# A block-sparse attention and expert-layer kernel on one core: mask step, a split cast and a new instruction order

## The chip, the cores and the metric

The kernel runs on one core of a Trainium2 chip. The metric is the device time of one execution in microseconds. The engines are TensorE (PE in the profile; PEld is its weight load), VectorE (DVE), ScalarE (ACT), GpSimd (POOL) and SyncE (SP), which only issues transfers here. Each engine works through its own instructions in the order of the program; they meet through semaphores.

## The reference, cut to what matters

```python
# 4 batches, 8 heads, 768 positions, head dimension 64; blocks of 32, so 24 blocks
scores = scale * q @ k.transpose(0, 1, 3, 2)
mask = abs(blk_i - blk_j) <= 1                       # the block's neighbours
mask |= (blk_i == 0) | (blk_j == 0) | (blk_i == 23) | (blk_j == 23)
for qb in range(24):                                 # three sampled blocks per query block
    for kb in sampled_blocks[qb]:
        mask[rows of qb, columns of kb] = True
attn = softmax(where(mask, scores, -1e9))
x = (attn @ v) as 3072 tokens x 512
h = x @ w_in                                         # 512 -> 1024
solu = h * softmax(h)
ln = (solu - mean) / sqrt(var + 1e-6) * g_ln
out = ln @ w_out                                     # 1024 -> 512
```

## The kernel before, in words

**Tiling.** Attention runs over 4 batches, 3 query tiles of 256 positions and 4 pairs of heads: 48 steps (`attend`). Each has three score groups (`score/b.t.pair.n`, L523: four matmuls of 256 columns into one of two `s` buffers of two banks each), three exps on ScalarE (`exp/...`, L528, 128 x 1024 each, into eight `ex` buffers) and one `pv` of 24 matmuls (L542). VectorE divides (`recip` L551, `norm` L554). A score group needs the transposed K and Q (`kT`, `qT`). The mask is added inside the score matmul: K and Q carry 24 extra rows, a selector of the key's block and -30000 where the query's block may not see that block.

**Opening and crossing.** For batch 0 (`opening`), SyncE loads K, Q and V of each pair (`load2` are 2 of the 6 chunks, `load4` the other 4, `load6` all), GpSimd or ScalarE casts them to bf16 next to the extra rows (`cast2`, `cast4`, `cast6`, L426), TensorE transposes them (`turn4`, `turn8`, L439) and VectorE copies the result out of PSUM (`evac4`, `evac8`, L426). `opening_rest` does the same for the other four chunks of Q (L484). Later batches (`crossed`) are cast by GpSimd (L495), transposed by a DMA that SyncE issues (`cross_kq`, L497) and split into `kT` and `qT` by VectorE (L501). GpSimd also casts V (L418).

**Expert layer.** Each of 24 feeds of 128 tokens (`feed`) does: two halves of `feed4` (L602, 512 columns), exp with its sum on ScalarE (`silu_e`, L624), the product on VectorE (`mult`, L627), statistics (`stats`, `aggr`), a small chain on GpSimd (`z2`, `vr`, `rs`: L640, L643, L676), a transposition of `u` by DMA (`cross_u`, L707) or on TensorE (first and last two), two halves of `out4` (L717), a scale by `rs` on VectorE (L723) and the store. Attention's result `x` is transposed by DMA (`cross_x`) or TensorE. The last two feeds are cut finer (`half_e`, `half_m`, `half_s`, `outh`), with a longer chain on GpSimd before `rs`.

**The mask step.** VectorE builds a 24 x 24 table of allowed block pairs: the fixed part (`allow0`, L280 and L282), then for each of the three samples one instruction that compares the block index with the sample and takes the maximum with the table so far (L287), the last of them writing `allow_b` in bf16. `maskmm2` and `maskmm4` (L305) spread it over positions, and L309 turns it into the extra rows of `qc` and `qr`.

**Order.** Nothing is scheduled automatically. Every operation is recorded in `Plan` in program order and numbered; `ORDER` lists the numbers in the order in which they are emitted, for all engines together, so it fixes each engine's queue. It also fixes which buffer of a pool an operation gets: the one that came free first. `SPARES` are matmuls of constants (L774) of the given column counts that compute nothing that is used; `ORDER` places them too.

Of the kernel before, what the change touches and what calls it, by code (L numbers as in the profile page):

```python
# [7 lines left out]
FP32 = mybir.dt.float32  # L8
# [6 lines left out]
SPARES = (512, 512, 512, 256, 256, 256, 256, 128, 128, 128, 128, 128, 128, 128, 128, 128, 128, 128, 128)  # L15
ORDER = [
# [107 lines left out]
def kernel(  # L124
# [11 lines left out]
    nc = tc.nc  # L136
# [678 lines left out]
```

## Time and profile before

| | |
|---|---|
| median of three runs | 207.87 us (207.56 to 208.7) |
| the profiled execution | 207.91 us |
| its span, first to last instruction | 206.2 us |
| TensorE busy | 198.3 us |
| ScalarE busy | 170.5 us |
| VectorE busy | 146.8 us |
| GpSimd busy | 73.0 us |
| moved by DMA | 41.29 MB |

The page gives an engine's busy time over the whole span; windows give it by stage. A timeline line has start, length, engine, line of the kernel, operation, output<-inputs, shapes and count; the bracket is the idle time of the engine ahead of it and what ended it. SPq is an issue on SyncE's queue, whose length is that of the issue alone. In a list of the chain of waits each line has start, length and what the chain ran through. A matmul's length holds its latency, so successive matmuls overlap: four score matmuls of 0.60 us follow each other every 0.44 us.

### The profile page before, as it was taken

The numbers are of one execution on the slowest core, as the hardware profiler recorded it, in microseconds if no ns is written. First come the engines' busy times: TensorE is split into PE (matmuls) and PEld (weight loads), VectorE is DVE, ScalarE is ACT, GpSimd is POOL, SyncE is SP. The second block draws the span as 40 slices with busy tenths as digits, with TensorE's granted clock in tenths as the row PEclk, the third lists the DMA queues.
The fourth block names the chain that finished last, engine by engine and source line by source line (L and its number), as shares of the span: only waits on it lengthen the run. The fifth ranks groups of instructions, "written<-read, shape, count | busy, mean of one in ns | idle before, by whom it ended". The sixth has DMA issues, their size and how long they took to land.

```text
span 206.2 us, 5792 instructions
## 1 busy us (share of the span) xinstructions
PE 198.3 (96%) x2292; PEld 141.3 (69%) x2292; DVE 146.8 (71%) x327; ACT 170.5 (83%) x210; POOL 73.0 (35%) x153
## 2 busy tenths in 40 slices
PE   3999999999999999999999999999999999999993
PEld 1888887677667667667666766666767676676452
DVE  6367489999897776877859374689586556459853
ACT  4298999999879898998888979998988999997570
POOL 6865423334516366311430415424120301200281
PEclk9999999999999999999999999999999999999999
DMA  4999999999999999999999969957972444342333
GB/s 134 294 333 373 283 285 253 257 216 223 162 315 305 280 198 278 197 328 207 281 294 184 227 181 279 177 130 80 209 163 51 103 104 80 79 105 51 74 118 120
DMA packets 71088, 41.29 MB, mean 200 GB/s; under 512 B 52236, under 2 KB 67092, under 8 KB 71060
## 3 DMA queue, kind: packets, MB, share of 16 engines
q1 hardware_dynamic: 69968, 39.86, 82.1%
q0 software_dynamic: 1056, 1.05, 3.0%
q8 instruction: 18, 0.29, 0.6%
q14 instruction: 10, 0.08, 0.2%
q10 hardware_dynamic: 36, 0.00, 0.0%
HBM read 23.07 MB, written 6.29 MB: 142 GB/s over the span
## 4 chain that ended last, share of the span: by engine, by line
PE 67%; DMA 15%; POOL 7%; issue 4%; DVE 4%; SPq 1%; ACT 0%; POOLq 0%; DVEq 0%; ACTq 0%
PE spairs L523 22%; PE mbank L717 16%; PE hpair L602 15%; PE mbank L542 12%; DMA qst<-in_q_dram 5%; DMA kst<-in_k_dram 4%; DMA vst<-in_v_dram 3%; DMA kx<-kb 3%; POOL kb L495 1%; PE sones L602 1%; SPq L497 1%; POOL va L418 1%; DVE u L654 1%; POOL rs L676 1%; DVE ot L723 1%
## 5 line engine op out<-in xcount | busy, mean ns | idle before, releaser
L528 ACT ACTIVATE ex<-spairs 128x1024 bf16<-128x1024 f32 x144 | 141.3, 1023 | 21.8 <-PE spairs L523 19.0
L523 PE MATMUL spairs<-qT,kT 88*128 88x256 bf16 x576 | 84.4, 274 | 0.9 <-ACT ex L528 0.6
L523 PEld LDWEIGHTS <-kT 88*128 88x128 bf16 x576 | 53.2, 98 | 21.6 <-issue 1.8
L717 PE MATMUL mbank<-w_out_sb,uT 128*128 128x512 bf16 x184 | 47.1, 379 | 0.0
L602 PE MATMUL hpair<-w_in_sb,xT 128*128 128x512 bf16 x176 | 45.0, 379 | 0.0
L542 PEld LDWEIGHTS <-ex 128*128 128x128 bf16 x1152 | 41.4, 97 | 4.7 <-DVE x L554 0.4
L542 PE MATMUL mbank<-va,ex 128*128 128x65 bf16 x1152 | 43.0, 193 | 0.0
L627 DVE TENSOR_TENSOR u<-hpair,e 128x1024 bf16<-128x1024 f32 x22 | 26.8, 1219 | 13.1 <-ACT e L624 12.9
L634 DVE BATCH_NORM_STATS2 bs<-u 128x6 f32<-128x512 bf16 x44 | 29.0, 678 | 0.2
L602 PEld LDWEIGHTS <-xT 128*128 128x128 bf16 x192 | 18.4, 97 | 13.7
L717 PEld LDWEIGHTS <-uT 128*128 128x128 bf16 x184 | 17.4, 97 | 13.5 <-DMA uT<-u 0.3
L723 DVE TENSOR_SCALAR ot<-mbank,rs 128x512 f32<-128x512 f32 x23 | 17.2, 747 | 11.2 <-POOL rs L676 6.9
L624 ACT ACTIVATE e<-hpair 128x1024 bf16<-128x1024 f32 x22 | 22.5, 1022 | 1.3 <-PE hpair L602 0.7
L643 POOL TENSOR_SCALAR vr<-z,mv 128x1 f32<-128x1 f32 x22 | 6.1, 280 | 44.9 <-DVE mv L637 35.2
L554 DVE TENSOR_TENSOR x<-mbank,r 128x256 bf16<-128x256 f32 x48 | 19.9, 414 | 0.8
L640 POOL TENSOR_TENSOR z<-z 128x1 f32<-128x1 f32 x22 | 4.2, 194 | 45.7 <-ACT e L624 41.3
L418 POOL CAST va<-vst 128x768 bf16<-128x768 f32 x16 | 14.6, 910 | 14.1 <-DMA vst<-in_v_dram 13.9
L551 DVE RECIPROCAL r<-mbank 128x4 f32<-128x4 f32 x48 | 8.4, 175 | 14.6 <-PE mbank L542 14.4
L676 POOL TENSOR_TENSOR rs<-vr,neg_half 128x1 f32<-128x1 f32 x24 | 13.5, 563 | 1.0
L495 POOL CAST qb<-qst 128x768 bf16<-128x768 f32 x12 | 10.2, 856 | 7.5 <-DMA qst<-in_q_dram 6.0
L495 POOL CAST kb<-kst 128x768 bf16<-128x768 f32 x12 | 10.4, 871 | 3.2 <-DMA kst<-in_k_dram 3.0
L501 DVE COPY kT<-kx 64x768 bf16<-64x768 bf16 x24 | 9.2, 383 | 2.2 <-DMA kx<-kb 1.8
(90 smaller groups left out, 122.6 us busy)
## 6 DMA issues: line engine op xcount, KB each, us to landing
vst<-in_v_dram SPq DMA_DIRECT2D x16, 384.0 KB, 5.2
out_dram<-ot SPq DMA_DIRECT2D x23, 256.0 KB, 3.0
kst<-in_k_dram SPq DMA_DIRECT2D x15, 384.0 KB, 4.7
qst<-in_q_dram SPq DMA_DIRECT2D x12, 384.0 KB, 4.8
w_out_f<-in_moe_w_out_dram SPq DMA_DIRECT2D x2, 1024.0 KB, 11.4
qst<-in_q_dram SPq DMA_DIRECT2D x4, 256.0 KB, 7.5
w_in_sb<-in_moe_w_in_dram POOLq DMA_DIRECT2D x2, 512.0 KB, 11.4
q0st<-in_q_dram SPq DMA_DIRECT2D x4, 128.0 KB, 3.9
```

What stands on the lines that cost most here:

```text
L418: ready_v[(b, pr)] = op(f"cast6/v{b}.{pr}", "POOL", lambda o: nc.gpsimd.tensor_copy(out=va[i][:, 2 * pr : 2 * pr + 2, :, 0:D], in_=vst[ld. ...
L495: ca = op(f"cast6/{nm}{b}.{pr}", "POOL", lambda o: nc.gpsimd.tensor_copy(out=cb[o.slot], in_=st[ld.slot].rearrange("p h c d -> p c h d")), ...
L523: nc.tensor.matmul(s[:, m, :], kT[0:KR, sl, jc, hh, :], qT[0:KR, sl, 2 * t : 2 * t + 2, hh, :], start=(m % 2 == 0), stop=(m % 2 == 1))
L528: exs.append(op(f"exp/{b}.{t}.{pr}.{n}", "ACT", lambda o, so=so: nc.scalar.activation(out=exb[o.slot], in_=banks("s", "pairs")[so.slot], f ...
L542: nc.tensor.matmul(acc(o)[:, qt, hh, :], exb[exs[n].slot][:, m, qt * P : (qt + 1) * P], va[i][:, 2 * pr + hh, jc, :], start=first, stop=(n ...
L554: nrm = op(f"norm/{b}.{t}.{pr}", "DVE", lambda o: nc.vector.tensor_tensor(out=xb[x_of[b, t].slot][:, :, 2 * pr * D : (2 * pr + 2) * D].rea ...
L602: nc.tensor.matmul(hb(n) if last else hb()[:, n, :], xTb[xt[0].slot][:, qt, c, :], w_in_sb[n][:, c, :], start=(c == 0), stop=(c == KD - 1))
L624: zs = op(f"silu_e/{j}", "ACT", lambda o: nc.scalar.activation(out=eb[o.slots["e"]], in_=hb().rearrange("p a f -> p (a f)"), func=ACT.Exp, ...
L627: us = op(f"mult/{j}", "DVE", lambda o: nc.vector.tensor_mul(out=ub[o.slot], in0=hb().rearrange("p a f -> p (a f)"), in1=eb[zs.slots["e"]] ...
L634: bs.append(op(f"stats/{j}.{n}", "DVE", lambda o, n=n: nc.vector.bn_stats(out=bsb[(bs[0] if bs else o).slot][:, n, :], in_=ub[us.slot][:, ...
L717: nc.tensor.matmul(mbank[m0.slot], uTb[ut[0].slot][:, KF // 2 * n + f, :], w_out_sb[n][:, f, :], start=(n == 0 and f == 0), stop=(n == 1 a ...
L723: fo = op(f"scale/{j}", "DVE", lambda o: nc.vector.tensor_scalar(out=otb[o.slot], in0=mbank[os_[0].slot], scalar1=rsb[rs.slot], scalar2=No ...
```

## The change

Three things change at once.

1. The mask table is built by two instructions instead of three: one comparison of the block index with all three samples (24 x 72 elements), written beside the fixed part into one bf16 tile, and one maximum over those four.
2. The second pair's K (batch 0, pair 1) is cast in two pieces on GpSimd, chunks 0 and 1 and then chunks 2 to 5, each with its own readers, where it was one cast of six chunks. For the pairs cast in one piece `ready_k` no longer names the first transposition for the second score group.
3. `ORDER` and `SPARES` are replaced: 14 spares of 4,352 columns instead of 19 of 4,096. Every operation keeps its engine.

```diff
-SPARES = (512, 512, 512, 256, 256, 256, 256, 128, 128, 128, 128, 128, 128, 128, 128, 128, 128, 128, 128)
+SPARES = (512, 512, 512, 512, 512, 256, 256, 256, 256, 256, 128, 128, 128, 128)
 ORDER = [
-    1124, 0, 21, 31, 1115, 2, 115, 11, 32, 1114, 3, 4, 5, 13, 33, 12, 14, 22, 15, 86, 9, 6, 16, 35, 23, 17, 18,
...
+    1120, 0, 5, 31, 2, 3, 30, 20, 21, 34, 23, 32, 4, 6, 13, 11, 9, 113, 17, 117, 10, 14, 22, 37, 12, 15, 115, 18,
...
 ]
...
-    allow = [const.tile([NB, NB], FP32, name=f"allow{i}") for i in range(3)]
+    allow = const.tile([NB, NR + 1, NB], BF16, name="allow")
...
-        out=allow[0], in0=dist, scalar1=1.0, scalar2=edge[1], op0=ALU.subtract, op1=ALU.is_le), [d2, e1])
-    static = op("small", "DVE", lambda o: nc.vector.memset(allow[0][:, 0 : NB : NB - 1], 1.0), [al0])
+        out=allow[:, NR, :], in0=dist, scalar1=1.0, scalar2=edge[1], op0=ALU.subtract, op1=ALU.is_le), [d2, e1])
+    static = op("small", "DVE", lambda o: nc.vector.memset(allow[:, NR, 0 : NB : NB - 1], 1.0), [al0])
...
-    prev, dep = allow[0], [static, iof, slo]
-    for r in range(NR):
-        nxt = allow_b if r == NR - 1 else allow[1 + r]
-        al = op("allow", "DVE", lambda o, r=r, prev=prev, nxt=nxt: nc.vector.scalar_tensor_tensor(
-            out=nxt, in0=iota_f, scalar=samp_f[:, r : r + 1], in1=prev, op0=ALU.is_equal, op1=ALU.max), dep)
-        prev, dep = nxt, [al]
+    eq = op("allow", "DVE", lambda o: nc.vector.tensor_tensor(
+        out=allow[:, 0:NR, :], in0=iota_f.rearrange("p (o b) -> p o b", o=1).broadcast_to([NB, NR, NB]),
+        in1=samp_f.rearrange("p (r o) -> p r o", o=1).broadcast_to([NB, NR, NB]), op=ALU.is_equal), [iof, slo])
+    al = op("allow", "DVE", lambda o: nc.vector.tensor_reduce(
+        out=allow_b, in_=allow.rearrange("p r b -> p b r"), op=ALU.max, axis=mybir.AxisListType.X), [eq, static])
...
+        elif (b, pr) == (0, 1):
+            ck = cast("POOL", kc, kst, 0, 2, lk, None, "kc", [lk], [lk])
+            cr = cast("POOL", kc, kst, 2, NCH, lk, ck, None, [lk], [lk])
...
-        ready_k[b, pr] = [[ga], [gr], [gr]] if first else [[ga], [ga, gr], [gr]]
+        ready_k[b, pr] = [[ga], [gr], [gr]]
```

By names, the start of three queues in the old and the new order:

```
TensorE before: spare128 spare512 spare512 maskmm2 turn4/k0.0 spare256 spare128 spare512 spare128 turn4/q0.0
                turn8/k0.2 spare128 turn4/q1.0 score/0.0.0.0 score/0.0.0.1 spare128 turn8/k1.2 turn4/k1.0
                score/0.0.0.2 turn8/k2.2 score/0.0.1.0
TensorE after:  spare256 turn4/k0.0 spare512 spare512 spare256 maskmm2 spare256 maskmm4 turn4/q0.0 turn8/k0.2
                score/0.0.0.0 turn4/q1.0 score/0.0.0.1 spare512 score/0.0.0.2 turn4/k1.0 turn8/k1.2 score/0.0.1.0
SyncE before:   k0(2) q0(2) k0(4) g q1(2) k1 k2 k3 v0 q2(2) q3(2) v1 q0(4) w_out q1(4) q2(4) v2 v3 k1.0 q3(4)
SyncE after:    q0(2) k0(2) q1(2) k0(4) q2(2) g q3(2) q0(4) k1 k2 v0 k3 v1 v2 w_out q1(4) v3 q2(4) q3(4) w_out k1.0
GpSimd after, from its first cast: q1(2) sel4 sel4 k0(4) maskc2 q2(2) q0(4) half maskc4 k1(2) k1(4) k2 v0 ... k3
```

In these lists `k1(4)` is the load or cast of four chunks of pair 1's K in batch 0, `k1` of all six, and `k1.0` the K of pair 0 in batch 1. Further on, the scores, exps and matmuls of the expert layer stand in nearly the same sequence; `out4/12` comes 732 ns of matmuls nearer to `feed4/12.1` (about 7.5 instead of 8.3 us of matmuls between them), and at the end `half_s/22.1` stands one place earlier on ScalarE and `rs/22` directly before `rs/23` on GpSimd, after `vr/23`.

102 rows, old and new, of the table ORDER are left out of this document.

## The prediction

> **What bounds the kernel now.** I read the page's busy shares and slices first, then the windows by stage, then the timeline of the first 26 us, the chain that ended last, and the timeline of the end.
>
> ```profile
> span 206.2 us, 5792 instructions
> PE 198.3 (96%) x2292; PEld 141.3 (69%) x2292; DVE 146.8 (71%) x327; ACT 170.5 (83%) x210; POOL 73.0 (35%) x153
> ...
> DMA  4999999999999999999999969957972444342333
> ```
>
> ```profile
> 9.40:33.70 24.30, 23.73 (x366) 20.77 (x364) 16.31 (x39) 22.55 (x26) 11.59 (x18) 1.00 1.10 302
> 33.70:57.00 23.30, 22.82 (x281) 16.40 (x280) 22.26 (x47) 21.62 (x27) 9.42 (x13) 1.00 1.13 227
> 57.00:190.00 133.00, 133.00 (x1539) 92.88 (x1536) 93.21 (x205) 117.43 (x138) 38.99 (x79) 1.00 0.85 189
> ```
>
> From 57 to 190 us TensorE is busy all 133 us: there the end moves only with TensorE's work, and the reordering changes none of it. Time can be won or lost in three places: before 57 us, where ScalarE (22.55 of 24.30 us) and the DMA engines (share 1.10) are nearly full too; at new holes between 57 and 190; and in the last 15 us.
>
> ```profile
> 1.30 0.45 SPq L332 DMA_DIRECT2D q0st<-in_q_dram  x1
> 3.65 0.50 DVE L287 SCALAR_TENSOR_TENSOR allow<-iota_f,samp_f,allow 24x24 f32<-24x24 f32 x2
> 4.18 0.23 DVE L287 SCALAR_TENSOR_TENSOR allow_b<-iota_f,samp_f,allow 24x24 bf16<-24x24 f32 x1
> 4.47 0.20 PE L305 MATMUL mbank<-allow_b,selp 24*128 24x24 bf16 x2 [2.52 <-DVE allow_b L287]
> ...
> 7.72 1.88 PE L523 MATMUL spairs<-qT,kT 88*128 88x256 bf16 x8
> ...
> 8.09 0.83 POOL L426 CAST kc<-kst 128x768 bf16<-128x768 f32 x1 [0.59 <-DMA kst<-in_k_dram]
> ...
> 8.81 4.17 ACT L528 ACTIVATE ex<-spairs 128x1024 bf16<-128x1024 f32 x4 [4.22 <-PE spairs L523]
> ```
>
> ```profile
> 11.96 2.85 ACT L528 ACTIVATE ex<-spairs 128x1024 bf16<-128x1024 f32 x3
> ...
> 17.82 1.04 PE L523 MATMUL spairs<-qT,kT 88*128 88x256 bf16 x8
> ```
>
> TensorE has nothing but spares until 4.47 us, then runs without a gap, but slowly: eight score matmuls take 1.88 us at 7.72 and 1.04 us at 17.82. The matmul records double their rate at 9.42. Exps follow each other every 0.915 us ((2.85 - 1.02) / 2). The 25th exp (third query tile, first pair) starts at 33.65, 24.84 us after the first; 24 x 0.915 = 21.96, so ScalarE waited 2.9 us in all. The second pair's K was issued at 3.19 and landed at 8.04.
>
> ```profile
> 15.60 9.73 DMA qst<-in_q_dram
> ...
> 29.40 8.46 DMA kst<-in_k_dram
> ...
> 48.09 6.09 DMA kx<-kb
> ```
>
> ```profile
> 200.61 0.56 POOL L676 TENSOR_TENSOR rs<-vr,neg_half 128x1 f32<-128x1 f32 x1
> 201.21 0.75 DVE L723 TENSOR_SCALAR ot<-mbank,rs 128x512 f32<-128x512 f32 x1 [1.51 <-POOL rs L676]
> ```
>
> The chain is transfers until 54 us, and TensorE's matmuls stand still for 0.11 us at 54.6 and 0.28 at 55.7 at its end. At the very end VectorE waits 1.51 us for `rs` of tile 22, and the last half product (`outh/1`) starts 0.5 us after `outh/0`'s last matmul for that.
>
> **The change part by part, against the profiled execution's 207.91 us (206.2 of span and 1.7 around it; the median of the three runs is 0.04 lower).**
>
> *Mask step: 0.* Three instructions of 0.23 us go. The new comparison has 72 elements a partition, between the 24x24 product at L274 (0.16) and twice L309's 96 elements (0.52); the maximum reads 96, likewise. Nearest is L309: 0.26 each. Together 0.3 to 1.0 us against 0.8, so `allow_b` comes between 0.5 us earlier and 0.3 later than 4.42. In the new order its first reader stands behind the first K transposition and three spares, 1,280 columns at the slow rate (0.107 us per 128): 1.07 us after about 5.05, so at 6.1. These hide either bound; without them the step would be worth its 0.5 or -0.3.
>
> *Order, first 12 us: +0.05 at the fourth exp.* SyncE now sends Q0 first, K0 second (issue 1.30; the second load landed at 4.17). K0's cast ends near 4.6 and TensorE starts at 4.65 with K0's transposition instead of the mask. Then 0.43 (four transpositions) + 1.07 (spares) + mask; `maskq` is 0.26 plus about 0.25 of latency, so Q0's transposition runs at 6.65 to 7.08, K0's other eight to 7.93 (0.85), first score at 7.93 against 7.72, first exp at 9.02 against 8.81 (1.09 after its score, as before). More hangs on the second K. `q0st` has two buffers, so Q2's load waits for Q0's cast (3.6) and Q3's for Q1's cast on GpSimd (about 5.0); Q3, the rest of Q0, K1 follow: K1 is issued at 5.95 instead of 3.19, and behind it in SyncE's queue K2, V0, K3, V1 all slide. Landing: small loads took 2.3 to 3.2 us, K1 4.85 and K2 5.32 in a full queue. With only 384 KB ahead I take 3.9: 9.85. GpSimd's two casts, 0.4 and 0.6 (L426 rows of 256 and 512 elements), end at 10.25 and 10.85; two transpositions, score, latency: 10.85 + 0.05 + 0.45 + 0.45 + 0.17 = 12.0 for the fourth exp, against 11.96. Cast in one piece (0.83) K1 would be done at 10.7, so the split itself is worth 0.1 either way.
>
> A page of the Trainium skill bears on that landing. "DMA: Bandwidth & Descriptors" (section "Anatomy of one DMA") gives about 2.0 us fixed plus bytes over 436 GB/s, so by an estimate from it K1 lands after 2.9 us, at 8.85, and nothing is late. The trace's 256 KB load took 3.16 where that gives 2.6; the row decides.
>
> *Order, 12 to 33 us: -0.6.* I walked scores, casts and evacuations with rows as above (score 0.44, 24 `pv` matmuls 0.73, eight transpositions 0.45, exp 0.915, slot of `s` free when the exp two back ends). K2 and K3 come 1.2 us apart behind K1, so exps 4 to 8 (from 0) are 0.3 to 0.6 late; but Q3's cast no longer stands on GpSimd behind the rest of Q0 (landed at 14.84, so Q3 was cast at 15.8 only; that rest now lands near 9), and exp 9 gets to 18.2 against 18.52; the last Q halves, in the queue ahead of the next batch (landed 25.3 before, about 22 now), keep exps within a few tenths of their cadence: exp 12 at 21.05 (21.34), 18 at 27.0 (27.57), 24 at 33.1 (33.65). Net -0.55 with the part above. Bounds: TensorE's own work up to there is 23.0 us (25 scores 10.9, seven `pv` 5.1, 96 transpositions 5.4, the rest 1.6), spares 1.5, cold loss 2.4, from 4.65: 31.6, so -2.0 at best; K1 landing after K2's 5.32 makes it +0.8 (the rival below).
>
> *Order, 33 to 57 us: -0.39.* The crossing of the next batch's first K starts later (its load now stands behind all Q of this batch; about 29.9 against 26.89), but the loads of K1 to K3 stand ahead of the crossings. Adding the durations of SyncE's entries (crossing 1.2 to 1.9, load 0.6) puts the last K crossing at 51.5 against 54.4, so the two holes go; 0 if not. `cross_u/2` falls behind it, ends near 58, and its reader is at 61.8.
>
> *57 to 190 us: +0.4.* `out4/12` stands 0.73 us of matmuls nearer to the feed whose transposed `u` it reads:
>
> ```profile
> 127.89 1.23 SPq L707 DMA_TRANSPOSE uT<-u  x1
> ```
>
> it landed at 132.92 and its reader started at 132.97, so up to 0.68 is lost, 0 if it takes 3.1 us like its quickest neighbours; I take 0.4, nearer to its own row. The other `out4` that come nearer (13, 15) had 1.8 and 2.1 us to spare.
>
> *End: -0.3.* `half_s/22.1` stands one place earlier on ScalarE, `rs/22` about 0.6 earlier on GpSimd, and then `out4/22.1` (over at 200.85) decides: between 0 and -0.5.
>
> Sum: -0.55 - 0.39 + 0.4 - 0.3 = -0.84: 207.07, or 207.0 beside the median.
>
> **The rivals.**
>
> *Larger gain, 205.8 us.* If K1 lands early in its bounds (9.2) and the Q halves as walked, the waits of ScalarE shrink by 1.7 of the 2.9 us, near TensorE's floor: -1.7 - 0.39 + 0.4 - 0.3 = -2.0. For it: the loads now go out in the order of their readers, and the waits are there to be had. Against: K1 is issued 2.8 us later.
>
> *Slower, 209.1 us: K1 comes late.* One mechanism: issued at 5.95 behind eight other loads, it takes K2's 5.32 us and lands at 11.3. Casts, transpositions and score put the fourth exp at 13.4, 1.4 late; TensorE is in order, so nothing else runs meanwhile. The 0.6 gained up to 33 us leaves +0.8; the late stream takes the -0.39 away, and `out4/12` costs its 0.68; the end gives -0.3: +1.2. For it: both rows of that size in the first 9 us. Against: those stood in a fuller queue, with seven loads issued in 3.4 us. It decides from a landing of about 10.5 on.
>
> *Hidden anyway, 207.6 us.* For it: the chain to 54 us is transfers, and as many bytes move. Against: SyncE's entries add up to an end 3 us earlier. If the last K crossing lands at 56.4 as before, the front's gain is given back there and the end's 0.3 alone is left.
>
> *The clock.* The slow stretch lasted 4.95 us from the first unbroken matmul. The Trainium skill ("TensorE: Matmul & The Clock Gate", section "What's actually happening") explains such a stretch by an activity window of about 3.4 us that runs freely and must be busy once, and leaves 3.4 to 6.8 us by an estimate; the row lies inside. It speaks against the change so far as 1,536 filler columns now stand between the first transposition and the first score, where 1,152 stood, all at the slow rate if the stretch lasts. From rows: 2 us more at half rate loses 1.0 us of matmuls, a third of it behind ScalarE, so about 0.6 more than the forecast, 207.6; I count it with the hidden case.
>
> **How the numbers follow.** Forecast 0.42 (its own range 206.3 to 207.8), larger gain 0.22, slower 0.24, hidden and clock 0.12. About 0.5% (1.04 us) is what a measurement can tell from no change: faster means below 206.83, slower above 208.91. The forecast's range gives 0.18 to faster and 0.24 to the same: faster 0.40, same 0.36, slower 0.24. The range 205.3 to 209.4 leaves a tenth beyond each side.
>
> **What would show it.** First score near 7.9, fourth exp at 12.0, exp 24 near 33.1; no hole at 55 us; a hole of under 0.7 us at `out4/12`; VectorE's last wait for `rs` under 1 us. The forecast is wrong if GpSimd waits for the second K past 10.5, or if TensorE shows holes in 60 to 190 us beyond that one.

## The result, and the profile after

| | before | after |
|---|---|---|
| median, runs of one comparison | 207.68 us (207.14 to 208.7, 6 runs) | 209.49 us (209.14 to 209.9, 6 runs) |
| the profiled execution | 207.91 us | 209.15 us |
| its span | 206.2 us | 207.4 us |
| first exp, fourth exp, exp 24 start at | 8.81, 11.96, 33.65 us | 9.10, 12.66, 33.78 us |
| from exp 24 to the end of the span | 172.55 us | 173.66 us |

The changed kernel takes 1.0081 times as long, with an interval of 1.0061 to 1.01: slower by about 1.7 us, where 207.0 us was forecast and 209.4 was the upper end of the range. A few executions of a kernel run slower as a whole and are marked so in the record; the medians and ratios below leave them out. Of the 1.24 us between the two profiled executions 0.13 lie ahead of exp 24 and 1.11 behind it.

The page of after, its first lines (busy time of each engine, share of the span, instructions):

```profile
span 207.4 us, 5744 instructions
PE 196.5 (95%) x2253; PEld 140.5 (68%) x2287; DVE 146.1 (70%) x326; ACT 170.0 (82%) x210; POOL 72.4 (35%) x154
```

TensorE's order has 2,287 matmuls (five spares fewer than before; the page counts as many weight loads) and the trace 2,253: 34 records are missing. Where one of 512 columns is missing, it leaves a gap of 0.22 us in TensorE's list that is no stop, and TensorE's busy time is short by it. The same stretches as before, in the view of windows (busy time and count for PE, PEld, DVE, ACT, POOL, then granted clock, DMA share, GB/s):

```profile
9.40:33.70 24.30, 23.76 (x360) 20.43 (x361) 17.37 (x38) 22.68 (x24) 12.74 (x19) 1.00 1.04 309
33.70:57.00 23.30, 22.20 (x268) 16.25 (x273) 22.65 (x46) 20.54 (x25) 7.85 (x12) 1.00 1.10 256
57.00:190.00 133.00, 131.01 (x1491) 92.16 (x1514) 90.49 (x201) 116.89 (x139) 38.64 (x82) 1.00 0.83 183
```

In the last row 48 matmuls fewer stand than before. Some of them are missing records, some were pushed out of the stretch; which, the busy time cannot say. So below a stop of TensorE is read from starts: the start of a matmul, less the start of the one ahead of it, less what that one's columns take.

The front of after, from the timeline (start, length, engine, line, operation, output<-inputs, shapes, count; in the bracket the idle time ahead and what ended it). The comparison is now L284, the maximum L287:

```profile
3.76 0.21 DVE L284 TENSOR_TENSOR allow<-iota_f,samp_f 24x72 bf16<-24x72 f32 x1
...
4.03 0.30 DVE L287 TENSOR_REDUCE allow_b<-allow 24x24 bf16<-24x96 bf16 x1
...
5.62 0.98 SPq L331 DMA_DIRECT2D kst<-in_k_dram  x2
...
6.02 0.22 PE L304 MATMUL mbank<-allow_b,selp 24*128 24x24 bf16 x2
...
8.00 1.06 PE L525 MATMUL spairs<-qT,kT 88*128 88x256 bf16 x4
```

```profile
10.13 0.96 POOL L425 CAST kc<-kst 128x256 bf16<-128x256 f32 x2 [0.76 <-DMA kst<-in_k_dram]
...
11.11 0.83 PE L438 MATMUL hfirst<-ident,kc 128*88 128x128 bf16 x12
11.53 1.13 DVE L425 COPY kT<-hfirst 88x512 bf16<-88x512 bf16 x2 [1.59 <-PE hfirst L438]
...
12.01 0.61 PE L525 MATMUL spairs<-qT,kT 88*128 88x256 bf16 x4
...
12.66 1.02 ACT L530 ACTIVATE ex<-spairs 128x1024 bf16<-128x1024 f32 x1 [0.33 <-PE spairs L525]
```

The mask table is done at 4.33 and read at 6.02, so that step is hidden. The second K lands at 10.08, its casts end at 11.09, and between its transposition (11.11) and its score (12.01) stands VectorE's copy out of PSUM (11.53). Four score matmuls of 1.06 us at 8.00 and 0.61 at 12.01 show the half rate at the start.

Now the place that costs most, 98 to 106 us in after, where the transposed `x` of token tile 10 is made:

```profile
98.18 1.06 SPq L728 DMA_DIRECT2D out_dram<-ot  x1
...
98.85 0.35 DVE L503 COPY kT<-kx 64x768 bf16<-64x768 bf16 x1
...
99.34 1.28 SPq L709 DMA_TRANSPOSE uT<-u  x1
99.80 0.40 DVE L556 TENSOR_TENSOR x<-mbank,r 128x256 bf16<-128x256 f32 x1
...
100.72 1.27 SPq L587 DMA_TRANSPOSE xT<-x  x1
...
101.53 0.35 DVE L503 COPY qT<-qx 64x768 bf16<-64x768 bf16 x1 [1.33 <-DMA qx<-qb]
...
102.30 1.23 DVE L629 TENSOR_TENSOR u<-hpair,e 128x1024 bf16<-128x1024 f32 x1
...
103.62 0.30 DVE L503 COPY kT<-kx 64x768 bf16<-64x768 bf16 x1
...
103.98 0.61 PE L525 MATMUL spairs<-qT,kT 88*128 88x256 bf16 x4 [0.18 <-DVE kT L503]
...
105.09 1.03 PE L604 MATMUL hpair<-w_in_sb,xT 128*128 128x512 bf16 x4 [0.50 <-DMA xT<-x]
```

The same two steps in before, the norm and the issue of the transposition:

```profile
97.60 0.41 DVE L554 TENSOR_TENSOR x<-mbank,r 128x256 bf16<-128x256 f32 x1
...
98.37 1.25 SPq L585 DMA_TRANSPOSE xT<-x  x1
```

Read the lines of after from the bottom. `feed4/10.0` (L604) starts at 105.09 because the transposition `cross_x/1.2` (L587) lands at 104.81. That was issued at 100.72, behind a store and `cross_u/8` on SyncE, and its input `x` is written only at 99.80 to 100.20 by `norm/1.2.3` (L556). Most of that delay is in the `pv` that the norm reads: `pv/1.2.3` starts its last matmul at 98.53, where before it was 96.69; the split at 98.85, which stands ahead of the division on VectorE, adds about 0.35. Before, the feed started at 103.10, 4.73 us behind the issue, and did not wait. A second chain at the same place: the score at 103.98 waits for a split (103.62) that stands behind the product (102.30), which stands behind a split that waits 1.33 us for a Q crossing. The stops, read from starts, are 0.34 us at 103.4 and 0.66 at 104.3. The chain that ended last (start, length, what it ran through) now goes through the transfer:

```profile
100.72 4.10 DMA xT<-x
105.09 1.67 PE hpair L604 x7
```

A third place, at 37 us. `kb` is the cast of the next batch's third K (`cast6/k1.2`), `kT` a split:

```profile
36.97 0.83 POOL L497 CAST kb<-kst 128x768 bf16<-128x768 f32 x1 [2.62 <-DMA kst<-in_k_dram]
...
36.99 1.38 DVE L503 COPY kT<-kx 64x768 bf16<-64x768 bf16 x2
...
38.30 1.21 DVE L629 TENSOR_TENSOR u<-hpair,e 128x1024 bf16<-128x1024 f32 x1
...
39.56 0.81 PE L604 MATMUL hpair<-w_in_sb,xT 128*128 128x512 bf16 x3 [0.36 <-DVE u L629]
```

Two splits take 1.38 us (the first 1.01, the second 0.35, as most do), the product behind them ends at 39.51, and `feed4/1.0` stops TensorE for 0.52 us (its records overlap, so the bracket shows less).

The end, which did gain:

```profile
201.67 1.07 POOL L678 TENSOR_TENSOR rs<-vr,neg_half 128x1 f32<-128x1 f32 x2
202.18 1.99 PE L737 MATMUL mbank<-w_out_sb,uT 128*128 128x256 bf16 x15
202.44 0.75 DVE L725 TENSOR_SCALAR ot<-mbank,rs 128x512 f32<-128x512 f32 x1 [0.87 <-POOL rs L678]
```

VectorE's last wait for `rs` is 0.87 us instead of 1.51, and the stop ahead of `outh/1` 0.19 instead of 0.51.

### The profile page after: what moved, and what is told of

Its sections match the earlier page's. It is cut to its first block, busy times and chain, and to the rows that moved or that the text cites. A ratio compares the mean times of both kernels' runs of the same rounds, so it can differ in the third digit from the quotient of the medians.

```text
span 207.4 us, 5744 instructions
## 1 busy us (share of the span) xinstructions
PE 196.5 (95%) x2253; PEld 140.5 (68%) x2287; DVE 146.1 (70%) x326; ACT 170.0 (82%) x210; POOL 72.4 (35%) x154
## 4 chain that ended last, share of the span: by engine, by line
PE 84%; DVE 8%; issue 2%; DMA 2%; POOL 1%; ACT 0%; POOLq 0%; ACTq 0%
PE spairs L525 27%; PE mbank L719 18%; PE hpair L604 16%; PE mbank L544 15%; PE hfirst L438 3%; DVE wsum L390 2%; DMA xT<-x 2%; DVE u L629 2%; PE sones L604 2%; DVE w_out_sb L404 1%; PE mbank L776 1%; PE mbank L737 1%; DVE x L556 1%; DVE kT L503 1%; PE mbank L577 0%
## 5 line engine op out<-in xcount | busy, mean ns | idle before, releaser
L719 PE MATMUL mbank<-w_out_sb,uT 128*128 128x512 bf16 x171 | 44.6, 379 | 0.6
L604 PE MATMUL hpair<-w_in_sb,xT 128*128 128x512 bf16 x157 | 42.6, 379 | 2.0 <-DMA xT<-x 0.5
L604 PEld LDWEIGHTS <-xT 128*128 128x128 bf16 x192 | 18.3, 97 | 14.9 <-issue 0.9
L725 DVE TENSOR_SCALAR ot<-mbank,rs 128x512 f32<-128x512 f32 x23 | 17.0, 740 | 6.1 <-POOL rs L678 3.7
L556 DVE TENSOR_TENSOR x<-mbank,r 128x256 bf16<-128x256 f32 x48 | 19.7, 414 | 0.9
L417 POOL CAST va<-vst 128x768 bf16<-128x768 f32 x16 | 13.1, 825 | 6.8 <-DMA vst<-in_v_dram 6.7
L503 DVE COPY qT<-qx 64x768 bf16<-64x768 bf16 x24 | 8.6, 359 | 2.1 <-DMA qx<-qb 1.9
## 6 DMA issues: line engine op xcount, KB each, us to landing
w_out_f<-in_moe_w_out_dram SPq DMA_DIRECT2D x2, 1024.0 KB, 11.3
```

What stands on the lines that cost most here:

```text
L556: nrm = op(f"norm/{b}.{t}.{pr}", "DVE", lambda o: nc.vector.tensor_tensor(out=xb[x_of[b, t].slot][:, :, 2 * pr * D : (2 * pr + 2) * D].rea ...
L604: nc.tensor.matmul(hb(n) if last else hb()[:, n, :], xTb[xt[0].slot][:, qt, c, :], w_in_sb[n][:, c, :], start=(c == 0), stop=(c == KD - 1))
L719: nc.tensor.matmul(mbank[m0.slot], uTb[ut[0].slot][:, KF // 2 * n + f, :], w_out_sb[n][:, f, :], start=(n == 0 and f == 0), stop=(n == 1 a ...
L725: fo = op(f"scale/{j}", "DVE", lambda o: nc.vector.tensor_scalar(out=otb[o.slot], in0=mbank[os_[0].slot], scalar1=rsb[rs.slot], scalar2=No ...
```

## The experiments

All have 6 to 12 runs, except j1 and j2 with one each, against the kernel before on the same chip (its median was 207.82 to 208.26 us there). "Old" and "new" order are those of before and after; every kernel has the new mask step and the split cast, so that names agree. Where two orders are joined at an entry, everything that the first emits up to it comes in the first's order, the rest in the second's; the text calls such a joint a seam.

| kernel | median us | ratio to before, 95% interval |
|---|---|---|
| e1: old order | 208.21 | 0.9997 [0.9971, 1.0023] |
| e2: new to 33 us, then old | 208.45 | 1.0004 [0.9984, 1.0025] |
| e3: old to 33 us, then new | 209.72 | 1.0082 [1.0051, 1.0114] |
| e4: new, `cross_x/1.2` mended | 209.08 | 1.0045 [1.0022, 1.0068] |
| f1: old, `cross_x/1.2` late | 211.46 | 1.0143 [1.0103, 1.0182] |
| f2: e4 and two more places | 209.35 | 1.0045 [1.0018, 1.0072] |
| f3: new to 65 us, then old | 210.09 | 1.0081 [1.0049, 1.0113] |
| f4: e2 with the new end | 208.15 | 0.9991 [0.9963, 1.002] |
| g1: after, casts halved | 209.65 | 1.0064 [1.0036, 1.0093] |
| g2: f4, casts halved | 208.77 | 1.0023 [0.9993, 1.0053] |
| g3: after once more | 211.16 | 1.0108 [1.006, 1.0155] |
| g4: f2 once more | 209.3 | 1.0032 [1.0006, 1.0058] |
| h1: new, old from 33 to 70 us, e4 behind | 210.35 | 1.0108 [1.0079, 1.0137] |
| h2: the same, after behind | 210.45 | 1.0122 [1.0081, 1.0163] |
| h3: f4 with K1 loaded early | 207.61 | 0.9989 [0.9962, 1.0016] |
| i1: old to 33 us, then f2 | 208.39 | 1.0039 [1.0013, 1.0066] |

### Which part: e1, e2, e3

e1 keeps the two small edits of the code and takes `ORDER` and `SPARES` of before; e2 and e3 join the two orders at `exp/0.1.3.2` (about 33 us), one way and the other.

> The changed kernel's mask step and split cast with the order and the spares of before (the comparison stands where the first of the three instructions stood, the maximum where the third stood, the two casts where the one stood). Theory of the holes (the 1.8 us are lost where transfers of the new order land late, at 39 and at 103 us, and in the first 30 us): within 0.4 us of before, 207.7. Rival, the two small edits cost something themselves: 0.5 us or more above before.

> The new order up to the exp of batch 0, tile 1, pair 3, group 2 (about 33 us), the old order for all that is left. Theory of the holes: the front costs 0.2 to 0.5 us, and the late first crossing, which is part of the front's load order, another 0.4: 208.2 to 208.6. Rival, the start (second K late, as in the slower case of the prediction) loses nearly all: 209.2 or more.

> The reverse: the old order up to that exp, the new order for the rest. Theory of the holes: 1.0 us lost at 103 us, 0.5 won at 55 us, 0.2 won at the end: 207.8 to 208.3. Rival, the start loses nearly all: 207.2 or less, since the end and the 55 us hole are won.

The mask step and the split cast are worth nothing that can be measured (e1). The new front alone costs nothing either (e2): in its profile exp 24 starts at 34.47 us, 0.8 later than before, and the stops from 33 to 58 us sum to 0.8 us instead of 1.5, the two at 54.6 and 55.7 being gone, so that the old order behind it takes most of the lateness up. And the new order behind 33 us costs as much as the whole change (e3, 1.0082 against 1.0081). The loss is made behind 33 us, by the order.

### One place: e4 and f1

e4 moves five entries of the new order, the division (`recip`, `norm`), the transposition and two splits:

```diff
- cross_u/8 split/k2.3.0 score/2.0.0.2 recip/1.2.3 ... norm/1.2.3 score/2.0.1.0 cross_x/1.2
+ recip/1.2.3 norm/1.2.3 cross_x/1.2 cross_u/8 split/k2.3.0 score/2.0.0.2 ...
- split/q2.3.0 score/2.0.1.1 ... split/k2.2.1 ... split/k2.2.0
+ split/k2.2.1 split/k2.2.0 split/q2.3.0 score/2.0.1.1 ...
```

> The new order with one place mended: the division of batch 1, tile 2, pair 3 goes ahead of the split of k2.3, the transposition of that x ahead of that of u8 on SyncE, and the splits of k2.2 ahead of that of q2.3. Theory of the holes: TensorE's stops at 103.4 and 104.3 us (0.3 and 0.7) go, 1.0 us less than the changed kernel: 208.4 to 208.7. Rival, the stop only moves on to the next feed or score, since VectorE is the one behind: 209.2 to 209.6.

In e4's timeline (an entry of SyncE's queue, then TensorE):

```profile
99.60 1.80 SPq L587 DMA_TRANSPOSE xT<-x  x1
```

```profile
103.78 0.60 PE L525 MATMUL spairs<-qT,kT 88*128 88x256 bf16 x4
104.22 1.46 PE L604 MATMUL hpair<-w_in_sb,xT 128*128 128x512 bf16 x6
```

The transposition lands at 103.71, and the feed follows its score after 0.44 us, which is the score's own length at full rate: no stop is left from 103 to 105 us. The ratio falls from 1.0081 to 1.0045. The two intervals overlap, so the 0.36% (0.75 us) is the best estimate and not a sharp one; the two stops of after that it removes sum to 1.0 us.

f1 goes the other way, with one entry of the old order:

```diff
- cross_x/1.2 scale/6 ... store/6 ... load6/q3.1 ... cross_u/8
+ scale/6 ... store/6 ... load6/q3.1 ... cross_u/8 cross_x/1.2
```

> The old order with one edit: the transposition of x for token tile 10 (cross_x/1.2) goes on SyncE's queue behind store/6, a Q load and cross_u/8 instead of directly behind its norm; everything else is e1's order. Theory (a transposition that is late for the feed that reads it stops TensorE one for one): in the profile of before this entry is issued at 98.37 and its reader starts at 103.10; behind cross_u/8 it is issued between 100.6 (if the entries ahead move up by its 1.25 us) and 102.0, needs 4.1 us as in the profile of after, so feed4/10.0 stops TensorE for 1.6 to 3.0 us and the time is 1.6 to 3.0 us above e1's, 209.8 to 211.2. Rival (such stops are made good later, because scores and ScalarE have slack): within 0.5 us of e1's 208.2.

```profile
100.83 1.23 SPq L709 DMA_TRANSPOSE uT<-u  x1
102.16 2.35 SPq L587 DMA_TRANSPOSE xT<-x  x1
```

```profile
106.69 1.04 PE L604 MATMUL hpair<-w_in_sb,xT 128*128 128x512 bf16 x4 [2.72 <-DMA xT<-x]
```

It was issued at 102.16, just past the late end of what was expected, and landed at 106.64. TensorE stopped for 2.9 us, and by the two ratios (1.0143 and 0.9997) f1 is 3.0 us slower than e1, the late end of what was expected: a transposition that is late for its feed costs its lateness in full here. Nothing behind it makes that good.

The profiles show the place more sharply than the times. The stops ahead of `score/2.0.2.0` and `feed4/10.0` sum to 1.0 us in after, 1.6 in e3 and 2.1 in g1, which all have the new order there; in e4, f2, g4, h1, i1, j1 and j2, which have e4's mend, there is none.

### The other half: f2, f3, g4, h1, h2, i1

f2 mends two more places of the new order on top of e4: k1.0's load one place earlier, and the VectorE piece `wo#2` behind the splits of pair 1.

```diff
- w_out#1 ... load6/k1.0
+ load6/k1.0 w_out#1
- wo#2 feed4/3.0 exp/1.0.0.1 split/k1.1.1 ... split/q1.1.1
+ feed4/3.0 exp/1.0.0.1 split/k1.1.1 ... split/q1.1.1 wo#2
```

> The new order with three places mended: as e4 around cross_x/1.2; the load of k1.0 (batch 1, pair 0) one place earlier on SyncE, ahead of the second half of w_out; one piece of folding the norm's weights into w_out (wo) behind the four splits of pair 1 instead of ahead of them on VectorE. Theory (what is left of the loss in e4 are the stops at 38.9, 0.55 us, and 51.7 with 52.4, 0.48 us): both go, and the time is about 0.8 us below e4's, 208.3, that is a ratio near 1.000 or a little below, since the end is 0.3 us better than the old order's. Rival (the stops are only where a shortage of transfers shows, and move on to the next reader): within 0.3 us of e4, ratio 1.004, with new stops of the same sum between 38 and 60 us.

> The new order up to exp/1.1.0.0 (about 65 us), the old one from there. Theory (half of the loss is made between 33 and 58 us): e2 lost nothing against before, and this differs from it only in 33 to 65 us, where the new order's stops at 36 to 39 and 49 to 52 us sum to 1.2 us more than e2's; so 0.9 to 1.2 us above e2: ratio 1.004 to 1.006. Rival (the loss is made behind 60 us alone): ratio 1.000 to 1.001.

The stops at 38.9 and 51.7 us are gone from f2's profile, and 0.40 us at 38.4 and 0.31 at 49.2 stand there; the stops from 33 to 58 us sum to 1.2 us where e4's sum to 1.9. But its ratio is e4's. So the rival was right on the time, and on the stops only in part: some went, others came. f3 lost 0.8% where 0.4 to 0.6 was expected, but its profile has stops of 0.38 us at 66.8 and 0.31 at 96.2 that neither before nor after has. Whether the seam makes them is open: f4, with no seam near, has 0.93 us ahead of the same feed at 95.8. f3 doesn't place the loss.

f2's profiled execution took 208.17 us, 1.2 us below its median, so a second one was taken of the same kernel:

> f2's kernel itself once more: its first profile was of an execution of 208.17 us, 1.2 us below the median of its runs, and showed no stop that before lacks. Theory (varying stops behind collisions make up what is left): a second profile of an execution near the median, 209 or more, shows 0.5 us or more of stops behind splits between 33 and 110 us that the first did not have. Rival (what is left lies in the start, in the clock or the first loads): no such stop, and the first exps are later by as much.

It took 209.61 us, and the rival was right for the larger part. The stops behind 33 us sum to within 0.4 us of f2's, but exp 24 starts at 35.21 us instead of 34.09, which is 1.1 of the 1.4 us between the two. GpSimd's casts of the second K (two pieces) and the third, first in f2's timeline, then in g4's:

```profile
9.64 0.96 POOL L425 CAST kc<-kst 128x256 bf16<-128x256 f32 x2 [0.64 <-DMA kst<-in_k_dram]
11.92 0.83 POOL L425 CAST kc<-kst 128x768 bf16<-128x768 f32 x1 [1.32 <-DMA kst<-in_k_dram]
```

```profile
10.21 0.96 POOL L425 CAST kc<-kst 128x256 bf16<-128x256 f32 x2 [0.55 <-DMA kst<-in_k_dram]
13.03 0.83 POOL L425 CAST kc<-kst 128x768 bf16<-128x768 f32 x1 [1.87 <-DMA kst<-in_k_dram]
```

The same load, issued at 6.09 and 6.78 us, landed at 11.77 in one execution and 12.89 in the other, and the fifth exp moved from 14.36 to 15.47. With the old front this K is issued at 3.7 us and landed between 8.8 and 9.4 in before, e1, f1 and i1, and the fifth exp started between 12.5 and 13.0.

h1 and h2 put the old order between 33 and 70 us (joined at `exp/0.1.3.2` and `exp/1.1.1.1`), with and without e4's mend behind it; i1 has one seam only, the old front, then f2's order.

> The new order up to exp/0.1.3.2 (33 us), the old one to exp/1.1.1.1 (about 70 us), the new one from there with the place around cross_x/1.2 mended as in e4. Theory (the other half of the loss is made by the new order as a whole between 33 and 70 us, whichever entry waits): nothing of the loss is left and the end is 0.3 us better, ratio 0.998 to 1.000, and exp 24 to exp 48 takes 30 us as in e2 and f4 (29.9) where f2 and e4 took 31.7 and 32.4. Rival (it is made behind 70 us, outside the mended place): ratio as e4 and f2, 1.003 to 1.0045.

> As h1, with the new order's own place around cross_x/1.2. Theory (that place is worth 0.7 to 1.0 us by itself): 0.7 to 1.0 us above h1, ratio 1.002 to 1.005, with stops of 0.7 to 1.0 us in all ahead of score/2.0.2.0 and feed4/10.0 near 103 to 105 us. Rival (the place costs only together with the late 33 to 60 us): as h1.

> The old order up to exp/0.1.3.2, behind it the new one with the place around cross_x/1.2 mended as in e4 and the piece of wo behind the splits of pair 1 as in f2 (K1.0 is loaded early in the old front anyway). Theory (the loss of the changed kernel is the place near 103 us, the stops at 36 to 53 us and a front 0.5 us late, less 0.3 us at the end): all three are gone here, exp 24 stands at 33.6 to 33.9 us, the stops between 33 and 58 us sum to no more than before's 1.5 us, and the time is as before or 0.3 us below, ratio 0.997 to 1.001. Rival (something in the new order behind 33 us costs half a per cent that no mended place holds): ratio 1.003 to 1.005, as f2 and g4.

h1 refutes its theory and its rival alike: 1.0108. Its profile has new stops around the second seam (0.29 us at 64.9, 0.16 and 0.48 at 74.4 and 75.1) and elsewhere (0.59 at 51.9, 0.47 at 99.3), so it doesn't place the loss. h2 lies 0.3 us above h1 (1.0122 against 1.0108), where 0.7 to 1.0 was expected, and well within the intervals: this pair of times shows neither the place nor its absence. i1's profiled execution is what the theory asked for: exp 24 at 33.27 us, stops of 1.6 us between 33 and 58 us, a span of 206.0 us, shorter than before's. But its ratio is 1.0039: its runs fall into six from 207.7 to 208.4 us and five from 209.1 to 209.7. Two more profiles were taken of it:

> i1's kernel once more, one execution. Theory (a stop that comes and goes with a collision of a split with a GpSimd cast, or with a transposition that lands late): if it takes 209 us or more, the profile shows one or two stops of together 0.9 to 1.3 us between 33 and 110 us that i1's first profile lacks, next to a split of over 0.6 us or a late transposition. Rival (the front varies by that much): exp 24 stands 0.9 us or more behind i1's 33.27, with the same stops behind it.

> As j1: a third profile of the same kernel. If it is of the lower group (below 208.5 us), the same stops as in i1's first profile, each within 0.15 us; if of the upper, as said for j1.

j1 took 208.9 us, j2 207.94. Between them lies no single stop and not the front (exp 24 at 33.48 and 33.32): j1 has 0.31 us at 43.7 that j2 lacks, 0.18 at 89.9, and 0.59 at 97.7 where j2 has 0.37. The last of these, in i1's first profile and then in j1's:

```profile
95.17 0.72 DVE L503 COPY qT<-qx 64x768 bf16<-64x768 bf16 x2 [0.22 <-DMA qx<-qb]
...
95.93 0.75 DVE L725 TENSOR_SCALAR ot<-mbank,rs 128x512 f32<-128x512 f32 x1
...
97.22 0.89 PE L544 MATMUL mbank<-va,ex 128*128 128x65 bf16 x24
```

```profile
96.83 0.72 DVE L503 COPY qT<-qx 64x768 bf16<-64x768 bf16 x2 [1.30 <-DMA qx<-qb]
...
97.58 0.75 DVE L725 TENSOR_SCALAR ot<-mbank,rs 128x512 f32<-128x512 f32 x1
...
98.39 0.89 PE L544 MATMUL mbank<-va,ex 128*128 128x65 bf16 x24 [0.43 <-DVE ot L725]
```

A Q crossing came later against the work around it (VectorE waits 1.30 us instead of 0.22), the scale behind the split (L725) went late with it, and `pv` waited for the PSUM bank which that scale frees.

### The end, the front, and collisions: f4, h3, g1, g2, g3

f4 is e2 with the new order again from `exp/3.2.3.2` on; h3 is f4 with one load moved:

```diff
- load2/q0.2 ... load2/q0.3 load4/q0.0 load6/k0.1
+ load6/k0.1 load2/q0.2 ... load2/q0.3 load4/q0.0
```

> The new order up to exp/0.1.3.2, the old one in the middle, the new one again from exp/3.2.3.2 to the end. Theory (the end of the new order is worth 0.3 us, since the stop ahead of outh/1 shrinks from 0.51 to 0.19 us; it was earned in the changed kernel and is buried under the loss in the middle): 0.3 us below e2, ratio 0.999, with the stop of 0.19 us in the profile. Rival (the end is set by another chain and the stop moves elsewhere in the last 12 us): ratio as e2's, 1.000 to 1.001.

> f4's order with the load of the second K (batch 0, pair 1) issued ahead of Q2's and Q3's first halves, near 3 us instead of 5.6; everything else as in f4. Theory (the late K1 is what makes the new front late): it lands near 8 us, the fourth exp moves from 13.28 in f4 to about 12.0, exp 24 from 34.40 to about 33.9, and the time falls 0.3 to 0.5 us below f4's, if nothing else in the front decides. Rival (in the new front TensorE's own order and its half-rate stretch decide, twelve K transpositions ahead of the scores of pair 1): the fourth exp stays past 12.5, exp 24 within 0.2 us of 34.1 to 34.4, and the time within 0.2 us of f4's.

The new end keeps its stop of 0.19 us in f4, h3 and i1, where before, e1, e2 and f1 have 0.50 to 0.51; 0.3 us is too little for the ratio to show. Loading K1 early didn't pull the front in: in h3 the fourth exp starts at 13.67 (13.28 in f4) and the time is as f4's within the intervals. In both the matmul records stay at half rate until 12.4 to 12.6 us, in h3 without a gap on TensorE from 4.85 on, and that decides there. Neither beats the kernel before by more than its interval.

g1 and g2 write GpSimd's casts of K and Q for batches 1 to 3, and of V, as two halves:

```diff
-ca = op(..., lambda o: nc.gpsimd.tensor_copy(out=cb[o.slot], in_=st[ld.slot].rearrange(...)), ...)
+ca = op(..., lambda o: [nc.gpsimd.tensor_copy(
+    out=cb[o.slot][:, 3 * i : 3 * i + 3], in_=st[ld.slot].rearrange(...)[:, 3 * i : 3 * i + 3]) for i in range(2)], ...)
```

> The changed kernel, with GpSimd's casts of K, Q (batches 1 to 3) and V written as two instructions of 384 elements instead of one of 768; order and engines as in the changed kernel. In the profiles so far a split that starts while such a cast runs ends 0.21 us after the cast's end, 0.6 to 1.0 us instead of 0.35. Theory (part of the loss that no place in the order shows comes from such collisions, with the product mult and then feed4 waiting behind the split): the longest split falls to about 0.65 us (half a cast, 0.45 to 0.5, plus 0.21), the stop at 38.9 us in the profile of after (0.52) falls below 0.2, and the time is 0.3 to 0.8 us below the changed kernel's in the same job. Rival (collisions are hidden behind other waits): within 0.3 us of it.

> f4's order (new front, old middle, new end) with the same halved casts. Theory (collisions): f4's profile had stops of 0.62 us at 64.0 and 0.93 at 95.8 behind splits of 0.88 to 0.99 us, and its runs spread from 206.8 to 211.4; with halves the stops behind splits stay below 0.4 us and the time is 0.3 to 1.0 us below f4's: ratio 0.994 to 0.998. Rival (hidden, or twice as many GpSimd instructions cost as much): ratio as f4's, 0.999 to 1.001.

> The changed kernel itself once more, as the baseline of g1 and for a second profile. Theory (places fixed by the order): the same stops as in its first profile, at 38.9 (0.5 us), 103.4 (0.34) and 104.3 us (0.66), each within 0.2 us; ratio 1.006 to 1.010. Rival (stops that vary with the transfers and collisions of an execution): the stop at 104 stays, since a queue sets it, but the one at 38.9 and others move or change by more than 0.3 us.

The longest split falls from 1.01 us to 0.67 in g1 and from 0.99 to 0.72 in g2, as expected, but two halves take about 1.0 us of GpSimd where one cast took 0.83 (GpSimd is busy for 80.1 us in g1 and 72.4 in after, with 40 casts cut in two). g2 is no faster than f4. g1 stands below g3, with intervals that overlap widely. So collisions of splits with casts are real, and that they cost time in sum is not shown. g3's one profile is of its longest execution, 213.79 us, and isn't read, so it doesn't answer whether after's stops stay where they are. e3 and g1 do for two of them: the stops near 104 us are there again, and the 0.52 us ahead of `feed4/1.0` is in neither.

## Why the prediction was wrong, step by step

Against the profiled execution of after, in us:

| step | forecast | measured | what was there |
|---|---|---|---|
| mask step | 0 | 0 | done at 4.33, read at 6.02; e1 |
| first 12 us (fourth exp) | +0.05 | +0.70 | 12.66 instead of 11.96 |
| 12 to 33 us | -0.6 | -0.57 | fourth exp to exp 24: 21.12 instead of 21.69 |
| 33 to 57 us | -0.39 | +0.5 | the two holes went, others came |
| 57 to 190 us | +0.4 | +1.0 | no stop at `out4/12`, 1.0 at `cross_x/1.2` |
| end | -0.3 | -0.3 | stop 0.19 instead of 0.51 |

The measured column sums to +1.3, and the span grew by 1.24. Three terms of the sum failed, by about 0.65 us (first 12 us), 0.9 (33 to 57) and 0.6 (57 to 190); together they are the 2.1 us between the forecast and the profiled execution.

*Wrong: "57 to 190 us: +0.4".* This is the step that failed where the experiments place the loss (e3, e4, f1). It priced one transposition, `cross_u/12`, which lost nothing (issued 129.88, reader at 134.72, no stop), and searched the `out4` for others. It left out the other kind. `feed4/10.0` had come nearer to the `pv` that its `x` comes from, 5.5 us of matmuls behind it instead of 6.4, while a split had been put ahead of its division and `store/6` and `cross_u/8` ahead of its transposition; the names in the two orders show both. e4 took that away and by the best estimate nearly half of the loss went; f1 made the transposition late in the old order and lost 3.0 us. The sentence that TensorE is busy all 133 us there and the reordering changes none of its work was right, and the conclusion that only new holes count was too. The holes had to be looked for at every reader of a transposition.

*Wrong: "first 12 us: +0.05".* K1 landed at 10.08, close to the 9.85 that was taken, and its casts ended at 11.09 instead of 10.85. But the chain written out (casts, transpositions, score, latency) leaves out VectorE's copy of the transposed K out of PSUM, which takes 0.41 to 0.42 us for 512 columns in both profiles. Together that is 0.66, and 0.65 was missing. The estimate set beside the sum, worked out from the Trainium skill ("DMA: Bandwidth & Descriptors", section "Anatomy of one DMA"), gave a landing at 8.85. That section gives its sum for transfers that GpSimd issues, and SyncE issued this one. The load took 4.46 us in after and 3.6 to 4.1 in e2, e4, f2, f3, f4 and g4: the trace does not agree with 2.9, and the row was the better guide.

*Wrong in its sign: "33 to 57 us: -0.39".* The two holes at 54.6 and 55.7 went, but not for the reason given, so the part that came out was luck. The sum of SyncE's entries put the end of the last K crossing at 51.5; its issue (`cross_kq/k1.3`) ended at 55.9 and it landed at 58.39, where before it was 54.4 and 56.41. TensorE only came to the holes later: `pv/1.0.0` starts at 55.78 instead of 54.94, and the last split that `score/1.0.2.0` reads ends at 56.34 instead of 56.02. e2 shows the same: its last K crossing lands at 56.42, as before, and its exp 24 is 0.8 late, so the holes close and most of the lateness is gone by 60 us. What the forecast did not have are new stops. GpSimd's cast of the next batch's third K, whose load had moved up (issued at 33.17 instead of 35.31), ran at 36.97 and met a split, and a product and a feed waited behind it (0.52 us); at 49.4 another 0.31 appeared.

*Right: 12 to 33 us and the end.* Both within 0.05 us. Exps 9, 12, 18 and 24 came 0.64 to 0.72 us behind the walk, that is by the error of the first 12 us and little more, though the last Q half landed at 24.7 and not near 22.

The rival on the slower side, 209.1 us, had nearly the right time for a wrong reason: it needed K1 to land at 11.3 and had its point of decision at 10.5; K1 landed at 10.08 and GpSimd had it from 10.13 on. The same mechanism did act on the third K in g4. By its own terms the larger gain comes to 205.9 us, not 205.8, which changes nothing here. Of the two signs named for a wrong forecast, the second came: TensorE has stops in 60 to 190 us beyond the one foreseen.

*What stays open.* About 0.4% is left in e4, f2, g4 and i1, with the late transposition mended and, in i1, the old front too. One small part is fixed: `score/3.2.1.0`, near 177 us, stops TensorE for 0.16 us in after, e3, e4, f2, g1, g4, h1 and i1, which have the new order there, and in none of before, e1, e2 and f1. In the better executions of f2 and i1 little is left of the rest (spans of 206.5 and 206.0 us against 206.2 before), so it lies mostly in how often the others come. g4 and j1 show two ways, a K load that lands 1.1 us later and a Q crossing that comes late. That the new order is met by these more often because it leaves transfers less room is an argument, not a finding: e1 and f4, with the old order in the middle, also had executions of 209.83 and 209.32 us, with stops of 1.2 us at 88.6 and 0.93 at 95.8.

## What to carry to other kernels

When an order is changed, list for each reader of a DMA transposition, whatever its kind, the work between the reader and the last instruction that the transfer needs, and compare it with the slowest such transfer in the trace: here 0.9 us less of it, and two queue entries put ahead, cost 1.0 us on an engine that was busy all the time. Write a chain out instruction by instruction; a copy of 0.4 us left out was most of the error of a step. And compare an order by several executions: one profile of the better kind showed i1 faster than before while its runs were 0.4% slower.

## What the runs showed of the hardware

**VectorE's splits and GpSimd's casts exclude each other.** In the profiles of after, e1 and f4 every split that began more than 0.01 us before the end of a running cast of 768 elements ended 0.21 us after that cast, whenever it had begun: in after the split at 36.99 began 0.02 us behind the cast, took 1.01 us and ended at 38.00, and the cast had ended at 37.80; the one at 104.88 took 0.82 and ended 0.21 us behind its cast. Where the split began first it kept its 0.35 us and the cast took up to 1.0 us instead of 0.82. The Trainium skill says the same ("SBUF — State Buffer", section "SBUF: two separate sides"): a port pair that the two engines share is a lock for the whole instruction, held by whichever starts first; on VectorE's side it names instructions in a two-port mode and some with two inputs in SBUF. The traces agree for these two instructions; splits that began while one of GpSimd's small operations (`rs`, `vr`, 128x1) ran still took 0.32 to 0.36 us.

**The half-rate start varies.** With the old front (before, e1, e3, f1, i1, j1, j2) the matmul records came to full rate between 8.4 and 9.6 us, with the new one (after, e2, e4, f2, f3, f4, g4, h1, h3) between 8.1 and 12.6, the first real matmul being at 4.3 to 4.9 us in all of them. A page named in the prediction, "TensorE: Matmul & The Clock Gate" of the Trainium skill (section "What's actually happening"), left 3.4 to 6.8 us for such a stretch by the estimate worked out there; e2's took 7.9 (4.54 to 12.42), so that bound does not hold here as it was worked out. The column of granted clocks shows 1.00 throughout, so it has to be read from matmul lengths.
